# A convolution and MLP kernel: a stream kept less its mean, 320-column banks, more split transforms and a seven-product block

## The chip, the cores and the metric

The kernel runs on one core of a Trainium2 chip. The metric is the device time of one execution in microseconds (us), the median of several runs. The engines are PE (matrix multiply, with PEld for its weight loads), DVE (vector), ACT (scalar), POOL and SP, which issues most DMAs.

## The reference, cut to what matters

```python
x = A_q                                        # 2048 tokens x 640 channels
x = x + A(layernorm(x), k, v, shift_k, ssm_k, ssm_D)
x = x + B(layernorm(x), w1, w2)
x = x + A(layernorm(x), k, v, shift_k, ssm_k, ssm_D)
x = x + B(layernorm(x), w1, w2)

def A(q, ...):
    kv = short_causal_conv(k, shift_k) * v     # 4 taps per channel
    y = causal_conv(kv, ssm_k) + kv * ssm_D    # 2048 taps per channel, over time
    return q * y                               # y does not depend on x
def B(x, w1, w2):                              # 640 -> 1728 -> 640
    return relu(x @ w1) @ w2
```

`y` is the same in both A layers, so it is worked out once.

## The kernel before, in words

**Chunks and blocks.** The 2048 tokens are 8 chunks of 256, each of two halves `s` of 128 tokens (half 1 holds the first 128 tokens in reverse). The MLP runs in blocks `(chunk, layer, halves)`. Chunks 0 and 1 run half by half; chunks 2 to 7 run with both halves in one block, in the order (2,0), (3,0), (2,1), (3,1), (4,0) and so on to (7,1). `main` (L913) emits a block, `prep` (L832) what stands ahead of it: for layer 0 and 1 the A part (statistics, gate with `y`, add) and the layernorm of B, then the split of the normed rows in two fp16 parts and their transposes.

**The MLP.** Each operand is a high and a low fp16 part, and three products (high by high, high by low, low by high) stand for one. `mm1` (L1009) makes `h`, 7 steps `j` of 256 hidden columns; ACT and DVE make relu and its two parts `hh`, `hl` (L1086, L1087); `mm2` (L992) adds into the output: per half one PSUM bank of 512 columns (`o0`, `o1`), and for the last 128 columns of both halves a third (`oc`). DVE adds the bank into the stream `x` (L1177, an instruction of 512 and one of 128 columns for each half). Blocks in `WINO`, which are (7,0), (6,1) and (7,1), use seven products of 320 columns in place of eight for the steps `j` that are not in `plain` (L941; `wprod` L970, `wplain` L959). For layer 0 of a chunk below 7 the first three `j` and the last tail step would be plain. The seven products need sums of quarters of w2 (`wcombine`, L750) and of `h` (L1073 to L1084), both made by ACT and DVE.

**The stream and layernorm.** `stats` (L782) makes the mean and the inverse deviation; ACT writes the normed rows `xn` (L810). For the A part DVE multiplies `xn` by `y` (L851) and adds that to `x` with a running sum (L855). Chunk 0 has a path of its own ("direct", L651 to L667), since its `y` stands at the head of everything.

**The convolution.** It is done chunk by chunk with transforms of length 128 on PE and complex products of chunk pairs on DVE. The work is cut into units of one or two (chunk, channel group) pairs; `SPLIT` says how many units of chunks 2-3, 4-5 and 6-7 take two channel groups of one chunk, the others take one channel group of two chunks ("chunk pairs"), which share the loaded partners. `transform` (L361) makes taps, product, and the transforms `pg` (of the filter) and `pr`; `products` (L550) the sums of products, the back transform `pq` and the store of `y`. A matmul of a transform is either fp32 (L471, L619) or "split": three products of a rounded high part and a rest (`mm3`, L326 to L330), for which ACT and DVE make both parts (L456, L457, L625, L626). `FG` and `FU` are the ranks in the list of units from which `pg` and `pq` are split; before, both are 11, which is the first unit of chunks 4-5.

**The order of the work.** `Plan.order` (L134) is a list scheduler. Each operation has an engine, a cost written by hand, and a class: `CRIT` (head of the kernel), `URGENT` (releases a block), `SOON`, `CONV`, `SPILL`, `LATER`, `FILL` (the MLP's matmuls). Each engine takes the lowest class that is ready and has room in its buffers, and the result is fixed as the engine's order of instructions. Any change of a cost or a buffer thus reorders much of the program. `T` makes a tile in a ring of buffers; the rings of PSUM are `h` (2 banks), `tr` (2, for the transforms), `o0`, `o1`, `oc` and `x` (1 each).

**The head.** While w1 and w2 stream in (28 tiles, L692), PE sums their squares (`pw`, L699) to find a scale for each (`norms`, L682: a diagonal `dg` L704, a small matmul `pn` L706, then `wn`, `wnr`, `wpw`, `wsc`). `wsplit` (L723) then makes the two fp16 parts of each of the 28 tiles, the high part on ACT (L731) and the low part on DVE (L732). "spin" matmuls (L716, L1194) fill PE where nothing else is planned.

Of the kernel before, what the change touches and what calls it, by code (L numbers as in the profile page):

```python
# [21 lines left out]
P = 128  # L22
# [37 lines left out]
FU = 11  # L60
FG = 11
SPLIT = (2, 0, 1)
HALVES = 2
AADD, RADD = (), ()
GADD, SADD = 4, 4
PAIRED = 1
WINO = ((7, 0), (6, 1), (7, 1))
# [8 lines left out]
class Tile:  # L76
    def __init__(self, ring, shape, dtype, name, stream=0):
        self.ring, self.shape, self.dtype, self.name, self.stream = ring, list(shape), dtype, name, stream
        self.t, self.left, self.writer, self.readers = None, 0, None, []
        if ring is not None:  # L80
            ring.lines.setdefault(stream, []).append(self)
# [4 lines left out]
    def r(self, pat, **kw):  # L86
        return self.t.rearrange(pat, **kw)

# [10 lines left out]
class Plan:  # L99
# [5 lines left out]
    def op(self, eng, cost, fn, reads=(), writes=(), prio=0, nbytes=0, late=0.0):  # L105
# [9 lines left out]
        for t in writes:  # L115
            if t.writer is not None:
                deps.add(t.writer)
            elif t.ring is not None and not t.left:
                o.new.append(t)
            deps.update(t.readers)  # L120
# [4 lines left out]
        o.tiles = list({id(t): t for t in (*reads, *writes)}.values())  # L125
# [8 lines left out]
    def order(self):  # L134
# [9 lines left out]
        def fits(o):  # L144
            at = {}
            for t in o.new:
                k = at.setdefault(t.ring, {})
# [14 lines left out]
        while n < len(self.ops):  # L162
# [27 lines left out]
            for e in engs:  # L190
# [17 lines left out]
                for t in best.new:  # L208
                    t.ring.free -= 1
# [23 lines left out]
    def issue(self):  # L233
        out, end = self.order()
        for o in out:
            for t in o.new:
                t.t = t.ring.pool.tile(t.shape, t.dtype, tag=t.ring.tag, name=t.name, bufs=t.ring.bufs)
# [5 lines left out]
def tile_h3_mlp(ctx: ExitStack, tc: tile.TileContext, q, kT, vT, shk, hF, hR, dD, w1, w2, cM, cG, out):  # L243
# [65 lines left out]
    POOL.memset(c15.t, 1.5)  # L309
    shs = keep(const, [P, NDT, 4], "shs")  # L310
# [22 lines left out]
    def pieces(u, ap):  # L333
# [23 lines left out]
        "p0": (ps, "o0", 1, 1),  # L357
        "p1": (ps, "o1", 1, 1),
    }

    def transform(u):  # L361
        ring = ALT if u == [(0, 2), (0, 3)] else MAIN

        def R(k, shape, name):
            pl, tag, bufs, stream = ring[k]
# [184 lines left out]
    def products(u, at, gt, after):  # L550
# [98 lines left out]
        act(h, lambda: ACT.activation(qs.t, pq[:, 256 : 256 + h].rearrange("p (a b) -> p a b", a=n), AF.Copy), [pq], [qs], pr_)  # L649
        pp = lambda: pq[:, 0:h].rearrange("p (a b) -> p a b", a=n)  # L650
        dve(h, lambda: DVE.tensor_sub(yo(0), pp(), qs.t), [pq, qs], [dst[0]], pr_)  # L651
# [11 lines left out]
        if direct:  # L663
            xs, xns, sp0 = first[c]
            for s in range(2):
                dve(h, lambda s=s: DVE.tensor_mul(xns[s][:, cs], xns[s][:, cs], dst[s][:, cs]), [xns[s], dst[s]], [xns[s]], (CRIT, BACK)[s])
                dve(h, lambda s=s: DVE.scalar_tensor_tensor(xs[s][:, cs], xns[s][:, cs], 1.0, xs[s][:, cs], op0=ALU.mult, op1=ALU.add, accum_out=sp0[s][:, 0, t0 // 2 : t0 // 2 + 1]), [xns[s], xs[s]], [xs[s], sp0[s]], (CRIT, BACK)[s], 0.2)  # L667
# [14 lines left out]
    def norms():  # L682
        ones = T(cv, "u", 2, [P, P], "ones", stream=1)
        plan.op("POOL", 0.5, lambda: POOL.memset(ones.t, 1.0), [], [ones], SOON)
        out_ = []
        for k, e in ((0, 9), (1, 13)):
            pw2 = T(ps, *(("h", 2), ("oc", 1))[k], [P, 2, P], f"pw{k}", stream=1)
            for j in JS:
                for i in range(2):
# [5 lines left out]
                    def f(m=2 * j + i, t=t, pw2=pw2):  # L695
                        top = t.t.bitcast(BF16).rearrange("p (n two) -> p n two", two=2)[:, :, 1]
                        for d in range(NDT):
                            x = top[:, d * P : d * P + P]
                            PE.matmul(pw2[:, 0], x, x, start=(m == 0 and d == 0), stop=(m == 2 * JS[-1] + 1 and d == NDT - 1))  # L699
# [4 lines left out]
            dve(P, lambda jk=jk, pw2=pw2, s2=s2: DVE.scalar_tensor_tensor(jk.t, pw2[:, 0], 1.0, ident.t, op0=ALU.mult, op1=ALU.mult, accum_out=s2.t), [pw2, ident], [jk, s2], URGENT, 0.2)  # L704
            pn = T(ps, "x", 1, [P, 512], f"pn{k}", stream=1)
# [73 lines left out]
    def small(tag, name):  # L779
        return T(mlp, tag, 2, [P, 2], name)  # L780

    def stats(xs, sums, name, S, pr=0, fine=False):  # L782
        q_ = slice(S[0], S[-1] + 1)
        negm, ssq, sd, r, v, nmr = (small(k, k + name) for k in ("negm", "ssq", "std", "rstd", "var", "nmr"))
        dve(2, lambda: DVE.tensor_scalar(negm[:, q_], sums[:, q_], -1.0 / D, None, op0=ALU.mult), [sums], [negm], pr)
        for s in S:
# [13 lines left out]
            (0.19 * len(S), [r, negm], [nmr], lambda: [A(nmr[:, c], r[:, c], ident_, scale=negm[:, c]) for c in cols]),  # L800
        ]
        if fine:
            for cost, rd, wr, f in steps:
                act(0, f, rd, wr, pr, cost - 0.1)
        else:
            act(0, lambda: [f() for *_, f in steps], [ssq, sd, negm, heps, c15], [v, r, nmr], pr, sum(x[0] for x in steps))
# [20 lines left out]
    def add_sum(x, t, sums, s):  # L827
        plan.op("POOL", 1.1, lambda: POOL.dma_start(out=x.t, in_=t.t, accum_op=ALU.add), [x, t], [x], URGENT, 8 * D * P)
        if sums is not None:
            act(D, lambda: ACT.activation(t.t, x.t, AF.Copy, accum_out=sums[:, s : s + 1]), [x], [t, sums], URGENT, 0.1)  # L830

    def prep(a, layer, S, pr=0):  # L832
# [4 lines left out]
        if head:  # L837
            xs, _, sp0 = first[a]
# [3 lines left out]
        else:  # L842
# [6 lines left out]
            xns = stats(xs, sums, "A" + nm, S)  # L849
            for s in S:  # L850
                ew("ay", D, lambda e, s=s, xn=xns[s]: e.tensor_mul(xn.t, ys[s].t, xn.t), [ys[s], xns[s]], [xns[s]], URGENT)  # L851
                if (a, layer) in AADD:
                    add_sum(xs[s], xns[s], sums2, s)
                    continue
                dve(D, lambda s=s, xn=xns[s]: DVE.scalar_tensor_tensor(xs[s].t, xn.t, 1.0, xs[s].t, op0=ALU.mult, op1=ALU.add, accum_out=sums2[:, s : s + 1]), [xns[s], xs[s]], [xs[s], sums2], URGENT, 0.2)  # L855
# [24 lines left out]
        else:  # L880
            xns = stats(xs, sums2, "B" + nm, S, pr)
        for s in S if not head else ():
# [16 lines left out]
        for x in range(2):  # L899
            pt = T(ps, f"o{x}", 1, [P, NDT, P], f"xt{nm}{x}", F16, stream=1)  # L900

            def f(x=x, pt=pt):
                for t in range(NDT):
                    PE.transpose(pt[:, t, :], hl[0][x][:, t * P : t * P + P], ident16.t)

            pe(0.29, f, [hl[0][x], ident16], [pt], pr)
            if x:
                dve(D, lambda pt=pt: DVE.tensor_copy(xt[1].t, pt.t), [pt], [xt[1]], pr)
            else:
                act(D, lambda pt=pt: ACT.activation(xt[0].t, pt.t, AF.Copy), [pt], [xt[0]], pr)  # L910
        return xT, S

    def main(n, a, layer, S, xTS):  # L913
# [7 lines left out]
        wino = (a, layer) in WINO  # L921
        if wino:
            bank = [T(ps, tag, bufs, [P, 512], f"o{n}{m}", stream=st) for m, (tag, bufs, st) in enumerate((("o0", 1, 0), ("o1", 1, 0), ("oc", 1, 0), ("x", 1, 3), ("tr", 2, 7), ("tr", 2, 7)))]
        else:
            ob = {s: T(ps, f"o{s}", 1, [P, 512], f"o{n}{s}") for s in S}
            oc = T(ps, *(("x", 1) if n == 1 else ("oc", 1)), [P, 2, P], f"oc{n}", stream=sm)
        o = lambda s, h: oc[:, s] if h else ob[s].t
        ds = (slice(0, H), slice(H, D)) if wino else (slice(0, 512), slice(512, D))
# [63 lines left out]
        def mm2(j, i, hh, hl, SS=S):  # L992
            tail = j == NFP - 1 and i == 1

            def f():
                wh, wl = (WT[j, 1, i][:, k, :] for k in range(2))
                for s in SS:
                    c = slice(i * R + (s - S[0]) * P, i * R + (s - S[0]) * P + P)
                    for h in range(2):
                        d, z = ds[h], o(s, h)  # L1000
                        end = j == JS[-1] and i == 1 and (h == 0 or s == S[-1])
                        PE.matmul(z, hh[:, c], wh[:, d], start=(j == JS[0] and i == 0 and (h == 0 or s == S[0])), stop=False)  # L1002
# [4 lines left out]
            pe(0.136 * (4 if tail else 6) * len(SS), f, [hh, hl, WT[j, 1, i]], [*(ob[s] for s in SS), oc], FILL)  # L1007
# [329 lines left out]
```

## Time and profile before

| | |
|---|---|
| median of 3 runs | 859.96 us (858.65 to 864.69) |
| span of the profiled execution | 858.4 us |
| busy: PE, DVE, ACT | 843.4, 743.1, 482.2 us |
| DMA, mean over the span | 207 GB/s, 178.05 MB |

The profiled execution's own time is its span and what little lies around it: the span is 0.3 us under the lowest of the three runs and 1.6 us under their median. Matmuls are pipelined: the page's duration of one is longer than the distance between the starts of two that follow each other, so what a matmul costs is read from the starts in the order of time.

### The profile page before, as it was taken

The numbers are of one execution on the slowest core, as the hardware profiler recorded it, in microseconds if no ns is written. First come the engines' busy times: TensorE is split into PE (matmuls) and PEld (weight loads), VectorE is DVE, ScalarE is ACT, GpSimd is POOL, SyncE is SP. The second block draws the span as 40 slices with busy tenths as digits, with TensorE's granted clock in tenths as the row PEclk, the third lists the DMA queues.
The fourth block names the chain that finished last, engine by engine and source line by source line (L and its number), as shares of the span: only waits on it lengthen the run. The fifth ranks groups of instructions, "written<-read, shape, count | busy, mean of one in ns | idle before, by whom it ended". The sixth has DMA issues, their size and how long they took to land.

```text
span 858.4 us, 19690 instructions
## 1 busy us (share of the span) xinstructions
PE 843.4 (98%) x7808; PEld 663.1 (77%) x7808; DVE 743.1 (87%) x1367; ACT 482.2 (56%) x1121; POOL 46.5 (5%) x57
## 2 busy tenths in 40 slices
PE   8989999999999999999999999999999999999997
PEld 7867877777878777777777777878777777888886
DVE  7999999999889999999999999999897575645543
ACT  6597586455686375728448383835416275727331
POOL 2000000000011001101010000001000000000000
PEclk9999999999999999999999999999999999999999
DMA  9994968798999979889788988687985562110100
GB/s 325 391 296 150 270 192 287 213 340 281 310 260 284 325 192 270 201 255 252 197 245 243 223 236 168 184 189 241 266 272 200 135 216 31 44 20 2 43 20 32
DMA packets 133838, 178.05 MB, mean 207 GB/s; under 512 B 50545, under 2 KB 87153, under 8 KB 133746
## 3 DMA queue, kind: packets, MB, share of 16 engines
q1 hardware_dynamic: 125426, 166.31, 62.5%
q0 software_dynamic: 8320, 10.49, 8.1%
q8 instruction: 61, 1.00, 0.5%
q14 instruction: 31, 0.25, 0.1%
HBM read 122.03 MB, written 34.08 MB: 182 GB/s over the span
## 4 chain that ended last, share of the span: by engine, by line
PE 81%; DVE 10%; DMA 4%; ACT 3%; issue 2%; SPq 1%; DVEq 0%; ACTq 0%
PE h L1030 12%; PE h L1033 12%; PE h L1031 12%; PE o L1003 8%; PE o L1002 8%; PE o L1005 7%; PE o L957 7%; PE oc L1003 2%; PE oc L1002 2%; PE oc L1005 2%; DMA A<-at 1%; PE pq L619 1%; DVE pd L596 1%; PE hb L1030 1%; PE hb L1031 1%
## 5 line engine op out<-in xcount | busy, mean ns | idle before, releaser
L1030 PE MATMUL h<-xT,w 128*128 128x256 f16 (+1 forms) x1290 | 301.5, 252 | 0.7 <-DVE hh L1087 0.6
L1033 PE MATMUL h<-xT,w 128*128 128x256 f16 (+1 forms) x1290 | 301.3, 251 | 0.4 <-DVE w L732 0.4
L1031 PE MATMUL h<-xT,w 128*128 128x256 f16 (+1 forms) x1290 | 301.3, 251 | 0.0
L1031 PEld LDWEIGHTS <-w 128*128 128x128 f16 x1390 | 136.0, 98 | 11.2 <-issue 1.0
L1030 PEld LDWEIGHTS <-w 128*128 128x128 f16 x1390 | 135.9, 98 | 10.4 <-ACT w L737 0.2
L1003 PE MATMUL o<-w,hh 128*128 128x512 f16 x364 | 137.9, 379 | 0.4 <-DVE w L732 0.4
L1002 PE MATMUL o<-w,hh 128*128 128x512 f16 x364 | 138.1, 379 | 0.0
L1033 PEld LDWEIGHTS <-w 128*128 128x128 f16 x1290 | 126.2, 98 | 9.8 <-DVE w L732 0.6
L597 DVE TENSOR_TENSOR pacc<-pacc,pd 128x768 f32<-128x768 f32 x140 | 133.0, 950 | 0.5
L1003 PEld LDWEIGHTS <-hh 128*128 128x128 f16 x728 | 71.2, 98 | 45.8
L1002 PEld LDWEIGHTS <-hh 128*128 128x128 f16 x728 | 71.2, 98 | 44.6 <-issue 0.2
L1086 ACT ACTIVATE hh<-h 128x512 f16<-128x512 f32 (+1 forms) x103 | 50.4, 489 | 97.7 <-PE h L1033 94.4
L1005 PE MATMUL o<-w,hl 128*128 128x512 f16 x234 | 88.7, 379 | 0.0
L1003 PE MATMUL oc<-w,hh 128*128 128x128 f16 x364 | 79.7, 219 | 0.0
L1002 PE MATMUL oc<-w,hh 128*128 128x128 f16 x364 | 79.7, 219 | 0.0
L596 DVE TENSOR_TENSOR pd<-Ax,Gx 128x768 f32<-128x768 f32 x83 | 77.8, 951 | 0.9 <-DMA Gx<-G 0.8
L1005 PEld LDWEIGHTS <-hl 128*128 128x128 f16 x468 | 45.8, 98 | 27.6
L1005 PE MATMUL oc<-w,hl 128*128 128x128 f16 x234 | 51.2, 219 | 0.0
L394 ACT ACTIVATE tp<-kt,shs 128x256 f32<-128x256 f32 (+1 forms) x78 | 42.7, 574 | 13.0 <-DVE acc L431 10.8
L1087 DVE SCALAR_TENSOR_TENSOR hl<-h,hh 128x512 f16<-128x512 f32 x55 | 37.6, 685 | 11.0 <-ACT hh L1086 11.0
L596 DVE TENSOR_TENSOR pd<-at,Gx 128x768 f32<-128x768 f32 x46 | 43.2, 951 | 0.6 <-DMA Gx<-G 0.5
L412 POOL DMA_DIRECT2D gs<-hr x20 | 19.6, 980 | 387.5 <-DVE pacc L593 189.1
(232 smaller groups left out, 1666.6 us busy)
## 6 DMA issues: line engine op xcount, KB each, us to landing
Ax<-A SPq DMA_DIRECT2D x89, 384.0 KB, 4.5
Gx<-G SPq DMA_DIRECT2D x89, 384.0 KB, 4.1
G<-gt SPq DMA_DIRECT2D x30, 384.0 KB, 5.2
A<-at SPq DMA_DIRECT2D x30, 384.0 KB, 4.6
y<-Y SPq DMA_DIRECT2D x30, 320.0 KB, 4.7
ws<-in_w SPq DMA_DIRECT2D x28, 320.0 KB, 6.6
x<-in_q SPq DMA_DIRECT2D x16, 320.0 KB, 5.5
out_dram<-x SPq DMA_DIRECT2D x16, 320.0 KB, 4.0
```

The costliest lines, as they stand in the source:

```text
L394: ACT.activation(o[:, i : i + m], kview(i, m, j), AF.Copy, scale=shs[:, t, j : j + 1])
L596: ew(f"mac{j % POOLMOD}", 768, lambda e, pd=pd, av=av, gv=gv: e.tensor_mul(pd.t, av(), gv()), [ax, gx], [pd], pr_)
L597: dve(768, lambda i=i, pd=pd: DVE.tensor_add(acc[:, i], acc[:, i], pd.t), [acc, pd], [acc], pr_)
L957: PE.matmul(b[:, c : c + w], x, y[:, z : z + w], start=done[i] == 1, stop=done[i] == total[i])
L1002: PE.matmul(z, hh[:, c], wh[:, d], start=(j == JS[0] and i == 0 and (h == 0 or s == S[0])), stop=False)
L1003: PE.matmul(z, hh[:, c], wl[:, d], start=False, stop=end and tail)
L1005: PE.matmul(z, hl[:, c], wh[:, d], start=False, stop=end)
L1030: PE.matmul(p[:, z], wh, xv(t, 0), start=b, stop=False)
L1031: PE.matmul(p[:, z], wh, xv(t, 1), start=False, stop=tail and e)
L1033: PE.matmul(p[:, z], wl, xv(t, 0), start=False, stop=e)
L1086: act(2 * R, lambda p=p, hh=hh: ACT.activation(hh.t, p.t, AF.Relu), [p], [hh], URGENT)
L1087: dve(2 * R, lambda p=p, hh=hh, hl=hl: DVE.scalar_tensor_tensor(hl.t, p.t, 0.0, hh.t, op0=ALU.max, op1=ALU.subtract), [p, hh], [hl], URGENT)
```

## The change

1. **Stream less its mean.** `x + xn * y`, with `xn = (x + negm) * r` (`negm` is minus the mean, `r` the inverse deviation), becomes `(x + negm) * (1 + r * y)`: ACT writes `1 + r * y`, one DVE instruction does the rest. The stream then lacks its mean, which is kept in small tiles (`MEAN`) and added back by ACT in layer 1 after the layernorm. The direct path of chunk 0 is changed in the same way, and `negm` moves from DVE to ACT.
2. **320-column banks.** `o0`, `o1`, `oc` and `x` become two rings `oA` and `oB` of one tile with two banks each; `mm2` writes 320 columns into either bank, and one DVE instruction of 640 columns adds both to the stream.
3. **`FU`, `FG` 11 to 8:** the last three units of chunks 2-3 use split transforms.
4. **`SPLIT` (2, 0, 1) to (2, 0, 0):** chunks 6 and 7 are all in chunk pairs.
5. **`WINO` gains (6, 0):** a fourth block with seven products, in the steps 3, 4 and 5 only (the rest is plain there). The units of chunk 7 and `wcombine` are now called for ahead of (6,0), no longer ahead of (7,0).
6. Options that were off (`AADD`, `RADD`, `add_sum`) are removed; the small rings get 4 buffers in place of 2.

```diff
-FU = 11
-FG = 11
-SPLIT = (2, 0, 1)
+FU = 8
+FG = 8
+SPLIT = (2, 0, 0)
...
-WINO = ((7, 0), (6, 1), (7, 1))
+WINO = ((6, 0), (7, 0), (6, 1), (7, 1))
...
+    def banks(tag, name, stream=0, shape=(512,), dtype=F32):
+        x = T(ps, tag, 1, [P, 2, *shape], name, dtype, stream)
+        return [Bank(x, k) for k in range(2)]
...
-        act(h, lambda: ACT.activation(qs.t, pq[...], AF.Copy), [pq], [qs], pr_)
-        dve(h, lambda: DVE.tensor_sub(yo(0), pp(), qs.t), [pq, qs], [dst[0]], pr_)
+        if direct:
+            xs, (negm, rs, nrs), qx, sp0 = first[c]
+            for s in range(2):
+                f = (nrs, rs)[s]
+                act(h, ... ACT.activation(qv(s), pm(), AF.Identity, scale=f[:, s : s + 1], bias=one.t), ..., (CRIT, BACK)[s], 0.09)
+                dve(h, ... DVE.scalar_tensor_tensor(qv(s), pp(), rs[:, s : s + 1], qv(s), op0=ALU.mult, op1=ALU.add), ..., (CRIT, BACK)[s], 0.13)
+                dve(h, ... DVE.scalar_tensor_tensor(xs[s][:, cs], xs[s][:, cs], negm[:, s : s + 1], qx[s][:, cs], op0=ALU.add, op1=ALU.mult, accum_out=...), ..., (CRIT, BACK)[s], 0.2)
+        act(h, lambda: ACT.activation(qs.t, pm(), AF.Copy), [pq], [qs], BACK if direct else pr_)
...
-        if direct:
-            xs, xns, sp0 = first[c]
-            for s in range(2):
-                dve(h, ... DVE.tensor_mul(xns[s][:, cs], xns[s][:, cs], dst[s][:, cs]), ..., (CRIT, BACK)[s])
-                dve(h, ... DVE.scalar_tensor_tensor(xs[s][:, cs], xns[s][:, cs], 1.0, xs[s][:, cs], ...), ..., (CRIT, BACK)[s], 0.2)
...
+        pw1, pn = banks("oB", "pw1", 2)
         for k, e in ((0, 9), (1, 13)):
-            pw2 = T(ps, *(("h", 2), ("oc", 1))[k], [P, 2, P], f"pw{k}", stream=1)
+            pw2 = pw1 if k else T(ps, "h", 2, [P, P], "pw0", stream=1)
...
-            pn = T(ps, "x", 1, [P, 512], f"pn{k}", stream=1)
...
-        dve(2, lambda: DVE.tensor_scalar(negm[:, q_], sums[:, q_], -1.0 / D, None, op0=ALU.mult), [sums], [negm], pr)
+        act(2, lambda: ACT.activation(negm[:, q_], sums[:, q_], AF.Copy, scale=-1.0 / D), [sums], [negm], pr, 0.1)
...
-                ew("ay", D, lambda e, s=s, xn=xns[s]: e.tensor_mul(xn.t, ys[s].t, xn.t), ..., URGENT)
-                dve(D, ... DVE.scalar_tensor_tensor(xs[s].t, xn.t, 1.0, xs[s].t, op0=ALU.mult, op1=ALU.add, accum_out=...), ..., URGENT, 0.2)
+                act(D, ... ACT.activation(qx.t, ys[s].t, AF.Identity, scale=r[:, s : s + 1], bias=one.t), ..., URGENT, 0.09)
+                dve(D, ... DVE.scalar_tensor_tensor(xs[s].t, xs[s].t, negm[:, s : s + 1], qx.t, op0=ALU.add, op1=ALU.mult, accum_out=...), ..., URGENT, 0.2)
+            keepm(a, negm, S)
...
+            if layer:
+                for s in S:
+                    act(D, lambda s=s: ACT.activation(xs[s].t, xs[s].t, AF.Identity, bias=MEAN[a][:, s : s + 1]), ..., URGENT, 0.1)
...
-            ob = {s: T(ps, f"o{s}", 1, [P, 512], f"o{n}{s}") for s in S}
-            oc = T(ps, *(("x", 1) if n == 1 else ("oc", 1)), [P, 2, P], f"oc{n}", stream=sm)
-        ds = (slice(0, H), slice(H, D)) if wino else (slice(0, 512), slice(512, D))
+        ob = {s: banks(("oA", "oB")[s], f"o{n}{s}") for s in S}
+        ds = (slice(0, H), slice(H, D))
...
-            for h in range(2):
-                    DVE.scalar_tensor_tensor(xs[s][:, d], o(s, h), fac[s].t, xs[s][:, d], op0=ALU.mult, op1=ALU.add, **acc)
+                DVE.scalar_tensor_tensor(xv_, ob[s][0].whole[:, :, 0:H], fac[s].t, xv_, op0=ALU.mult, op1=ALU.add, **acc)
```

More of the change, by code (lines that the diff above doesn't have):

```diff
@@ L805, in stats @@
         else:
[L806 removed]
+            act(0, lambda: [f() for *_, f in steps], [ssq, sd, negm, heps, c15], [v, r] + [nmr] * (nmr is not None), pr, sum(x[0] for x in steps))
+        if gate_:
+            return negm, r, nmr
         xns = {}
```

139 lines of the change are left out of this document (79 added, 60 removed).

## The prediction

> **What bounds the kernel now.** First the page: the span, the busy shares and the slices.
>
> ```profile
> span 858.4 us, 19690 instructions
> PE 843.4 (98%) x7808; PEld 663.1 (77%) x7808; DVE 743.1 (87%) x1367; ACT 482.2 (56%) x1121; POOL 46.5 (5%) x57
> DVE  7999999999889999999999999999897575645543
> ```
>
> PE is busy for 843.4 of 858.4 us, so 14.9 us are left in which it has nothing to do. The view by stretches tells where they lie (columns: stretch, its length, then PE, PEld, DVE, ACT, POOL busy, the granted clock, the DMA share, GB/s).
>
> ```profile
> 0.00:20.00 20.00, 16.66 (x112) 15.09 (x113) 13.87 (x29) 12.44 (x27) 4.37 (x17) 1.00 0.92 320
> 20.00:40.00 20.00, 19.35 (x243) 18.17 (x242) 18.15 (x58) 10.06 (x26) 0.00 (x0) 1.00 1.04 389
> 40.00:60.00 20.00, 17.77 (x237) 14.69 (x237) 19.35 (x38) 19.61 (x39) 0.00 (x0) 1.00 1.03 345
> 60.00:80.00 20.00, 19.19 (x209) 13.99 (x207) 19.86 (x43) 15.21 (x30) 0.00 (x0) 1.00 0.38 125
> 140.00:160.00 20.00, 19.57 (x226) 16.03 (x224) 18.92 (x36) 13.97 (x37) 0.00 (x0) 1.00 0.73 234
> 160.00:180.00 20.00, 17.92 (x196) 14.13 (x195) 18.92 (x32) 7.01 (x17) 0.00 (x0) 1.00 0.97 308
> 220.00:840.00 620.00, 619.94 (x5405) 480.31 (x5403) 527.76 (x927) 335.96 (x780) 40.24 (x38) 1.00 0.68 189
> 840.00:858.40 18.40, 13.09 (x129) 10.88 (x126) 8.48 (x20) 2.67 (x5) 0.00 (x0) 0.94 0.10 37
> ```
>
> PE idles 3.34 + 0.65 + 2.23 + 0.81 = 7.0 us before 80, 0.43 + 2.08 = 2.5 us between 140 and 180, 0.06 us in the 620 us from 220 to 840, and 5.3 us at the end, where the last block is added and stored. So three limits follow each other: the head, where DVE is at 18 to 19.9 of 20 us; the long middle, where only matmul work counts; and an end that the change leaves alone (the instruction order of both programs ends with the same operations). In the middle a microsecond taken from DVE or ACT is worth nothing by itself. What is worth something is a matmul less.
>
> **The change part by part: matmul work.** The price of a matmul is the distance between starts. In order of time (start, length, instruction):
>
> ```profile
> 205.98 1.08 PE L619 MATMUL pq<-u,cM 128*128 128x256 f32 x4
> 206.90 0.38 PE L1002 MATMUL o<-w,hh 128*128 128x512 f16 x1
> ...
> 313.24 0.28 PE L329 MATMUL pq<-ul,cMh 128*128 128x256 f32 x1
> 314.41 0.27 PE L330 MATMUL pq<-uh,cMl 128*128 128x256 f32 x1
> ...
> 654.63 0.38 PE L1002 MATMUL o<-w,hh 128*128 128x512 f16 x1
> 655.44 0.38 PE L1002 MATMUL o<-w,hh 128*128 128x512 f16 x1
> ...
> 732.70 0.43 PE L957 MATMUL o<-wt,hh 128*128 128x320 f16 x2
> 732.97 0.30 PE L957 MATMUL o<-wt,hl 128*128 128x320 f16 x1
> ```
>
> *Split transforms.* An fp32 matmul leaves two records; four of them, two matmuls, take 0.92 us up to the next start, 0.46 a matmul, in which the change from one kind to another is counted; I take 0.43, the lower end. The split form takes three: from 313.24 to 314.41 lie ten steps, 0.117 each, so 0.35. Three units, two transforms each (`pg` and `pq`), four matmuls each: 24 x (0.43 - 0.35) = **-1.9 us** (-2.6 by 0.46). DVE pays for it with 12 more differences of 512 (0.684 each, below: +8.2 us), ACT with 12 more casts; they fall between 150 and 240 us, where PE's only idle of the middle lies, and are weighed there.
>
> *320-column banks.* A pair of 512 and 128 columns three times over takes 655.44 - 654.63 = 0.81, so 0.27 for a pair; 320 columns take 0.27 / 2 = 0.135, so two of them 0.27. **0 us** on PE; the number of matmuls is the same.
>
> *Seven products in (6,0).* In the steps 3, 4 and 5, 24 matmuls of 320 columns become 21: 3 x 3 x 0.136 = 1.2 us less; 38 more of the matmuls that are cut in 192 + 128 columns cost some 3 ns each: **-1.1 us**. The work that it adds on DVE (per step four sums of 128, two differences; then some 12 instructions in place of two to empty the banks) comes to about 12 us and lies in the stretch where the page's slices show DVE at half load (the last ten slices).
>
> *Chunk pairs for 6 and 7.* Same five units, same matmuls; 24 loads of 384 KB fewer. DMA is no limit in that stretch: **0 us**.
>
> **DVE and ACT work.** Rows of the groups by shape (busy us, mean ns behind the bar):
>
> ```profile
> L851 DVE TENSOR_TENSOR xnA<-y,xnA 128x640 f32<-128x640 f32 x30 | 24.0, 820 | 3.4 <-ACT xnA L810 2.4 <-DMA y<-Y 0.9
> L626 DVE TENSOR_TENSOR ul<-u,uh 128x512 fp32r<-128x512 f32 x20 | 13.7, 684 | 0.7 <-ACT uh L625 0.6
> L1177 DVE SCALAR_TENSOR_TENSOR x<-o,winv,x 128x512 f32<-128x512 f32 x24 | 17.9, 745 | 2.4 <-PE o L1005 2.4
> L1177 DVE SCALAR_TENSOR_TENSOR x<-oc,winv,x 128x128 f32<-128x128 f32 x24 | 8.3, 345 | 2.3 <-PE oc L1005 2.3
> L773 DVE SCALAR_TENSOR_TENSOR wt<-wc,wsc,wt 128x1280 f16<-128x1280 f32 x4 | 6.2, 1552 | 4.4 <-ACT wt L772 4.4
> ```
>
> 30 products of 0.82 go (-24.6). 745 and 345 ns lie 384 columns apart, 1.04 ns a column, so one of 640 takes 0.88 in place of 1.09: with two halves fewer, -7. `negm` moves to ACT (-5). Against it +8.2 (split) and +12 (seven products): DVE loses about 17 us of 743. ACT gains 16 adds of a mean (about 0.9 each by L810's kind of instruction) and the casts, and stays under two thirds. By the bound above none of it counts from 220 on. From 80 to 220 DVE has some 10 halves of A parts at -0.8 and the narrower emptying at -0.2, against +8.2 for the splits, so a little is won, and I take **-0.8 us** of the 2.5 us idle there. Ends: +2 (the splits push `hl` back and PE waits as at 160 to 180 once more) and -2.5 (all idle goes).
>
> **The head.** What starts block (0,0) are the transposed rows and the first split tiles of w1:
>
> ```profile
> 35.82 0.15 DVE L710 TENSOR_SCALAR wsc<-wpw 128x1 int32<-128x1 int32 x1
> 36.75 0.55 DVE L865 TENSOR_SCALAR xc<-x,negmB 128x640 f32<-128x640 f32 x1
> 38.94 0.29 DVE L704 SCALAR_TENSOR_TENSOR dg<-pw,ident 128x128 f32<-128x128 f32 x1 [1.64 <-PE pw L699]
> 41.07 0.88 DVE L869 SCALAR_TENSOR_TENSOR xl<-xc,rstdB,xh 128x640 f16<-128x640 f32 x1
> ...
> L732 DVE SCALAR_TENSOR_TENSOR w<-ws,wsc,w x28: 867/878/885, 39.2 to 71.3; 128x640 f16<-128x640 f32 x28
> ...
> 42.29 0.22 PE L1018 MATMUL h<-xT,w 128*128 128x128 f16 x1
> ```
>
> The direct path needs two DVE instructions after ACT for half 0 in place of three, and the work for `y` itself is put behind; `cMl`, the first `dg` and one sum no longer stand in DVE's way. By the order, `xc` comes about 2 us earlier, at 34.6. But the order also puts the `pn` matmul of w1 behind the last `pw` of w2, which waits for the last weight tile (38.9 here), and DVE takes `wn`, then the second `dg`, before `xl` and before w1's scale. So the scale, at 35.82 before, comes at about 40.5; then ACT makes the first high part (0.8), the copy of the transposes, the second high part, DVE the low parts: the first `mm1` starts near 43.8 in place of 42.3, **+1.5**. Then DVE has 28 splits of 0.80 (22.4) and 12.6 us of other work in its order up to the last split, 35.0 us from 38.9: last split out at about 74, before 72.1. That it does not cost 2 us more is due to the order on PE: the transforms of chunk 1 (`pg`, 1.7 us) and two steps of `mm1` for half 1 (3.4 us), whose rows are ready earlier, now stand between the first `mm1` and the `mm2` that wait for w2's splits. Going down PE's order with these times, it has done the same amount of matmul work at 79.7 as before at 80.9: **-1.2 us** for the whole head. Ends: +4 (the first matmul late and nothing won back) and -4 (also the idle between 40 and 80 shrinks by most of its 3.0).
>
> **Sum.** -1.9 - 1.1 - 0.8 - 1.2 = -5.0: the profiled execution's 858.4 becomes 853.4. It lies 1.6 us under the median of 859.96, so I forecast **855.0** (-0.6%). A measurement of this kernel can tell about 1% from no change.
>
> One rule speaks against the split. Loading a matrix of 128 columns for it has this row:
>
> ```profile
> L330 PEld LDWEIGHTS pq<-uh,cMl x40: 187/188/189, 313.2 to 676.9; 128*128 128x128 f32 x40
> ```
>
> [...] By weight loads the split costs: 12 loads of 0.188 per transform against 8 of 0.190, +0.74 us x 6 = +4.4 us. The trace does not agree that loads set the pace here: split matmuls start 0.117 apart, less than one load lasts, and LDWEIGHTS is busy for 77% while PE's starts leave no gap.
>
> **The rivals.**
> 1. *Weight loads bound PE* (the rule just weighed): the split then gives +4.4 in place of -1.9. 855.0 + 6.3 = 861.3. Against it stand the starts 0.117 apart in 313 to 314. Chance 0.03.
> 2. *The head gets slower* (the other side). DVE's order puts `wn`, which waits for the last weight tile, ahead of all it needs for block (0,0). If PE cannot use the other work in between, because `h` has only two banks and its reader `hl` stands behind the splits on DVE, then the end of the splits sets the head: +1.9 there and another +1.5 to 3 of PE's wait for the first `mm1`, about +4.5. 855.0 + 5.7 = 860.7. It decides from a head 3.8 us longer than before. For it: DVE at 19.35 of 20 from 40 to 60. Chance 0.12.
> 3. *The matmuls saved come back as waits*: 8 us more DVE work between 150 and 240, where DVE has 18.9 of 20, makes `pg` and `hl` late. +3 in place of -0.8: 858.8. Chance 0.17.
> 4. *DVE's relief clears the idle time*: all of the 2.5 us, and 3 more of the head. 855.0 - 1.7 - 3 = 850.3. For it: both stretches wait on DVE. Against it: the first wait of the head is one for DMA. Chance 0.14.
> 5. *(6,0) waits for its sums*: `wcombine` (six times four sums of 0.49 and one row L773, 21 us of DVE) must be done by step 3 of (6,0). By the order, PE has 71 us of work between the last `pq` and that step, so it should fit; if not, some 10 us: 865 to 870. Chance 0.04.
>
> **How the numbers follow.** The forecast has 0.50. Its own range is 852 to 857.5. The range from 850 to 861 takes in rivals 2, 3 and most of 4, with the bounds of the head (+4, -4) and of the middle. Faster by over 1% means under 851.4: most of rival 4 and a little of the forecast, 0.16. Slower by over 1%, over 868.6: part of rival 5 and what I do not see, 0.05. Within 1%: 0.79.
>
> **What would show it.** Right: 12 split matmuls at 0.117 apart for units of chunks 2 and 3; PE idle of 0.1 us or less per 100 us after 240; the first `mm1` of block (0,0) near 43.8 and PE idle before 80 at 6 to 8 us; PE's busy time near 840. Wrong: a first `mm1` after 46, PE waits on `hl` or `pg` between 150 and 240 of over 4 us, or gaps in block (6,0).

## The result, and the profile after

The changed kernel takes 857.84 us in the median of 20 runs (856.51 to 861.41), the kernel before, run beside it, 860.85 (858.65 to 864.69): ratio 0.9965, 95% interval 0.9956 to 0.9974, or 3.0 us less. 855.0 had been forecast (-0.6%), with 850 to 861 as range.

The page of the changed kernel begins so:

```profile
span 856.9 us, 19812 instructions
PE 842.0 (98%) x7878; PEld 710.7 (83%) x7878; DVE 731.4 (85%) x1295; ACT 505.3 (59%) x1188; POOL 47.0 (5%) x58
```

This execution took 859.45 us, 1.6 more than the median; why is seen in the head below. DVE lost 11.7 us (17 forecast). PEld, the weight loads, is busy for 48 us more while the time fell, and split matmuls still start 0.12 us apart (below): rival 1 is out. The stretches that answer to those shown of before:

```profile
0.00:20.00 20.00, 17.13 (x111) 15.16 (x112) 13.72 (x28) 12.53 (x29) 4.74 (x18) 1.00 0.91 316
20.00:40.00 20.00, 18.51 (x202) 16.60 (x201) 18.64 (x56) 10.10 (x30) 0.00 (x0) 0.96 1.04 391
40.00:60.00 20.00, 19.11 (x271) 17.41 (x270) 17.70 (x37) 17.95 (x36) 0.00 (x0) 0.95 0.91 297
60.00:80.00 20.00, 20.00 (x207) 16.29 (x205) 19.73 (x37) 16.93 (x31) 0.00 (x0) 1.00 0.46 173
140.00:160.00 20.00, 19.22 (x217) 16.23 (x216) 19.94 (x36) 15.16 (x38) 0.00 (x0) 1.00 0.86 284
160.00:180.00 20.00, 19.69 (x225) 17.13 (x223) 20.00 (x33) 8.63 (x19) 0.00 (x0) 1.00 0.95 311
220.00:840.00 620.00, 617.81 (x5444) 516.40 (x5443) 517.10 (x873) 353.38 (x827) 42.26 (x40) 1.00 0.65 175
840.00:856.90 16.90, 11.63 (x113) 9.52 (x110) 8.54 (x20) 2.29 (x5) 0.00 (x0) 0.92 0.10 39
```

PE's idle time went from 7.0 to 5.25 us before 80, from 2.5 to 1.1 between 140 and 180, stayed at 5.3 in the end, rose from 0 to 1.1 between 80 and 140, and rose from 0.06 to 2.2 us in the long middle from 220 on, which was forecast to stay as it was. Two columns are new there: the granted clock (the third last) is 0.96 and 0.95 in the head, and DVE is at 19.94 and 20.00 of 20 us from 140 to 180.

To compare the work itself I value every matmul by its distance to the next start where nothing waits (0.056 us for 128 columns, 0.136 for 320, 0.118 for a split one of 256, two records of 0.216 for one in fp32) and add up all of them: 833.4 us before, 830.4 after, **2.9 us less** before rounding, against 3.0 forecast. The split matmuls come as forecast, here in a `pg` at 162 us:

```profile
162.90 0.28 PE L355 MATMUL pg<-gh,cGl 128*128 128x256 f32 x1
163.02 0.28 PE L353 MATMUL pg<-gh,cGh 128*128 128x256 f32 x1
163.14 0.28 PE L354 MATMUL pg<-gl,cGh 128*128 128x256 f32 x1
163.26 0.28 PE L355 MATMUL pg<-gh,cGl 128*128 128x256 f32 x1
```

So the time fell by 3.0 us and the matmul work by 2.9, which looks like an answer: only matmul work counts. The experiments show that it is a coincidence of larger terms.

**The wait in the middle.** PE's longest wait after 80 us, with ACT's and POOL's instructions around it (the brackets hold the idle time ahead of an instruction and what ended it):

```profile
269.16 0.75 ACT L421 ACTIVATE tp<-kt,shs 128x512 f32<-128x512 f32 x1
272.66 0.63 ACT L438 ACTIVATE hr<-hr 128x512 f32<-128x512 f32 x1 [2.76 <-DMA gs<-hr]
273.20 0.37 ACT L1132 ACTIVATE hh<-h 128x256 f16<-128x256 f32 x1
```

```profile
264.65 0.91 POOL L439 DMA_DIRECT2D gs<-hr  x1 [1.56 <-issue]
```

```profile
273.62 0.31 PE L1048 MATMUL o<-w,hh 128*128 128x320 f16 x1 [1.55 <-ACT hh L1132]
```

L438 changes the sign of `hr` in place and has to wait for the accumulating transfer that reads `hr`; issued at 264.65, it lets L438 start at 272.66, 8 us later, where the planner's model has 1.1 us after its bytes. The `hh` that PE needs wants nothing from that transfer; it only stands behind L438 in ACT's queue. PE idles 1.55 us for it, 1.7 counted between undisturbed starts.

### The profile page after: what moved, and what is told of

Read it like the earlier page. It is cut to its first block, busy times and chain, and to the rows that moved or that the text cites. A ratio compares the mean times of both kernels' runs of the same rounds, so it can differ in the third digit from the quotient of the medians.

```text
span 856.9 us, 19812 instructions
## 1 busy us (share of the span) xinstructions
PE 842.0 (98%) x7878; PEld 710.7 (83%) x7878; DVE 731.4 (85%) x1295; ACT 505.3 (59%) x1188; POOL 47.0 (5%) x58
## 4 chain that ended last, share of the span: by engine, by line
PE 74%; DMA 8%; DVE 8%; ACT 6%; issue 2%; SPq 1%; DVEq 0%; POOLq 0%; ACTq 0%
PE h L1076 11%; PE h L1077 11%; PE h L1079 11%; PE o L1003 9%; PE o L1048 8%; PE o L1049 8%; PE o L1051 7%; DMA ws<-in_w 2%; DMA gs<-hr 2%; DMA gs<-in_hF 1%; DMA hf<-in_hF 1%; PE hb L1077 1%; PE hb L1076 1%; DVE pd L623 1%; DVE w L763 1%
## 5 line engine op out<-in xcount | busy, mean ns | idle before, releaser
L1048 PE MATMUL o<-w,hh 128*128 128x320 f16 x672 | 200.3, 299 | 1.6 <-ACT hh L1132 1.6
L1049 PE MATMUL o<-w,hh 128*128 128x320 f16 x672 | 200.0, 299 | 0.4 <-DVE w L763 0.4
L1077 PEld LDWEIGHTS <-w 128*128 128x128 f16 x1390 | 136.0, 98 | 15.1 <-issue 1.2
L1051 PE MATMUL o<-w,hl 128*128 128x320 f16 x416 | 124.4, 299 | 0.0
L1132 ACT ACTIVATE hh<-h 128x512 f16<-128x512 f32 (+1 forms) x100 | 48.4, 484 | 66.7 <-PE h L1079 57.1
L1048 PEld LDWEIGHTS <-hh 128*128 128x128 f16 x672 | 65.7, 98 | 24.2 <-ACT hh L1132 1.9
L1049 PEld LDWEIGHTS <-hh 128*128 128x128 f16 x672 | 65.8, 98 | 21.8
L1051 PE MATMUL o<-w,hh 128*128 128x320 f16 x208 | 62.2, 299 | 1.0 <-DVE hh L1133 0.9
L1051 PEld LDWEIGHTS <-hl 128*128 128x128 f16 x416 | 40.7, 98 | 15.8
L1003 PE MATMUL o<-w,hh 128*128 128x192 f16 (+2 forms) x312 | 42.2, 255 | 0.0
L1133 DVE SCALAR_TENSOR_TENSOR hl<-h,hh 128x512 f16<-128x512 f32 x52 | 35.6, 685 | 5.7 <-ACT hh L1132 5.4
L1119 ACT ACTIVATE ha<-h 128x512 f32<-128x512 f32 x20 | 11.8, 589 | 48.0 <-PE h L1079 48.0
L1123 DVE TENSOR_TENSOR hs<-ha 128x128 f32<-128x128 f32 x20 | 5.8, 290 | 38.5 <-ACT ha L1119 38.5
```

Of the source, the lines that this page charges most:

```text
L1003: PE.matmul(b[:, c : c + w], x, y[:, z : z + w], start=done[i] == 1, stop=done[i] == total[i])
L1049: PE.matmul(z, hh[:, c], wl[:, d], start=False, stop=end and tail)
L1051: PE.matmul(z, hl[:, c], wh[:, d], start=False, stop=end)
L1077: PE.matmul(p[:, z], wh, xv(t, 1), start=False, stop=tail and e)
L1132: act(2 * R, lambda p=p, hh=hh: ACT.activation(hh.t, p.t, AF.Relu), [p], [hh], URGENT)
L1133: dve(2 * R, lambda p=p, hh=hh, hl=hl: DVE.scalar_tensor_tensor(hl.t, p.t, 0.0, hh.t, op0=ALU.max, op1=ALU.subtract), [p, hh], [hl], URGENT)
```

## The experiments

Theory A, which takes from the prediction the terms that add up to the measured 3.0: only matmul work counts; the gain is the split's 1.9 and block (6,0)'s 1.1. Rival B: the gain is DVE's relief between 80 and 220 us. All ratios are to the kernel before on the same chip.

**1 to 3: the parts one by one.** Edits of the changed kernel:

```
e1  FU, FG = 11, 11                            (no more split units)
e2  WINO = ((7, 0), (6, 1), (7, 1))            (block (6,0) by eight products)
e3  both of these, and SPLIT = (2, 0, 1)       (stream and banks alone)
```

> The changed kernel with the three more units back in fp32 (FU and FG 11); the other parts stay. Theory A (only matmul work counts: the gain of 3.0 us, from 860.85 to 857.84, is the split's 1.9 and block (6,0)'s 1.1): the sum of matmul work rises by 1.9 us and the time goes to 859.8, a ratio to the kernel before of 0.9987. Theory B (the gain comes from DVE's relief in 80 to 220 us, and the split uses part of it up as waits): without the split's 12 differences there is less waiting, and the time stays at 857.8 or falls, ratio 0.9965 or less.

> The changed kernel with block (6,0) by eight products again; the other parts stay. Theory A: matmul work rises by 1.1 us and the time goes to 858.9, ratio 0.9978; the wait of 0.62 us at 687 us goes, so 858.3 if that wait was due to the sums. Theory B: the seven products in (6,0) gave nothing, since DVE's sums before them cost what they save: 857.8, ratio 0.9965.

> The stream less its mean and the 320-column banks alone: no further split, old units for chunks 6 and 7, block (6,0) by eight products. Theory A: matmul work is that of the kernel before; DVE's 25 us less count for nothing in the middle, and the head is as long as before: ratio 1.000 (0.999 to 1.001), 860.8. Theory B: DVE's relief is worth 1.5 us or more in 80 to 220 us: ratio 0.998 or less.

Measured: e1 858.22 us, 0.9954 (0.9941 to 0.9967); e2 858.12, 0.9965 (0.9952 to 0.9979); e3 858.59, 0.9963 (0.9950 to 0.9976). The stream and the banks alone give the whole gain, though their matmul work, 833.4 us, is that of the kernel before. Theory A falls. e1 comes out as its theory B has it (0.9965 or less), and e2 at the number of its own: the 1.1 us of block (6,0) do not show in the time, within an interval of about 1.1 us to either side. The stream and the banks are not told apart by any run. Yet the 2.9 us less are there in the changed kernel: so something in it takes them back. e1 and e3 have the instruction order of the changed kernel up to about 150 us and a new one from there on, e2 up to block (6,0). Of e2, which has the split, the waits of PE and of ACT between 262 and 280 us (total, times, longest):

```profile
PE o L1048 <- ACT hh L1132: 1.6, 1, 1.6
```

```profile
ACT hr L438 <- DMA gs<-hr: 2.8, 1, 2.8
```

In e1 and e3, without the split, that view lists no wait of PE and none of L438. So the split's 1.9 us seem to come back as the wait at 273 us; e6 and e10 test that.

**4: w1's scale early.** `pn` of w1 ahead of the last eight weight tiles' `pw`, by one dependency more:

```
-                    pe(5 * 0.057, f, [t], [pw2], SOON)
+                    pe(5 * 0.057, f, [t] + [pn] * (k == 1 and j in JS[-2:]), [pw2], SOON)
```

> The changed kernel with one dependency more, which puts the pn matmul of w1 ahead of the last eight weight tiles' pw matmuls, so that w1's scale no longer waits for w2's last tile. Theory C (the late scale makes the head 2.5 us longer than it need be): scale near 38.5 in place of 41.3, first mm1 near 42.5 in place of 44.9, and the time falls by 2 us, to 855.8, ratio 0.9942. Theory D (other work on PE and DVE's chain of splits cover it, the head is bound by DVE until 74 us): first mm1 earlier, PE work done at 80 us the same within 0.5, time 857.8, ratio 0.9965.

Measured: 859.51, 0.9977 (0.9968 to 0.9985), slower than the changed kernel. Its profile can't be set beside the others, so where the time lies isn't shown; e11 tries the same again.

**5: the product back.** One instruction more in each A part:

```
+ dve(D, lambda qx=qx: DVE.tensor_tensor(qx.t, qx.t, qx.t, op=ALU.max), [qx], [qx], URGENT)
```

> The stream and the banks alone (as in e3, ratio 0.9963), with one DVE instruction of 640 columns more in each half of every A part outside the head: a maximum of q with itself, which changes no value and stands in place of the product that the stream took away (30 times 0.82 us, 24.6 us of DVE). Theory B (the gain of 3.0 us is DVE's relief outside the head, in 80 to 220 us): DVE is back at about 742 us and the time at 860.5, ratio 0.999. Theory E (the gain is in the head, where this instruction does not stand, or in the banks): time as in e3, 858.6, ratio 0.9963; lost time of PE before 80 us about 10 us, after it as in e3.

Measured: 865.99, 1.0045 (1.0026 to 1.0064): 7.4 us over e3, where B had 860.5, 1.9 over it. The direction is that of B, the size is almost four times its own. The planner gives every engine a new order for it, and the longest wait is one that e3 does not have:

```profile
PE h L1077 <- DMA xT<-xh: 2.3, 1, 2.3
```

**6 to 8: three edits by way of the planner.** e6 tells the planner that an accumulating transfer takes 7 us; e7 and e8 put six spins behind the last `pw` steps, e8 with e4's dependency.

```
e6  -  end = dma + 1.1
    +  end = dma + (1.1 if e == "SP" else 7.0)
e7  +  for _ in range(6 * (k == 1 and j in JS[3:])):
    +      PE.matmul(spin2[:, 0:P], ident16.t, ident16.t, start=True, stop=True)
    ...    (the step's price in the plan rises to match)
```

> The changed kernel, with the order's model of an accumulating transfer on POOL's queue set from 1.1 to 7 us after its bytes, so that ACT's L438, which waits for the first one, is put behind more of the hh that PE needs. In the changed kernel and in e2 (both with the split) PE waits 1.7 us at 273 us for an hh that stands behind L438; in e1 and e3 (both without) it does not. Theory F (the split's 1.9 us are real, and come back as this wait): the wait goes, and the time falls by 1.7 us against the changed kernel, to 856.1, ratio 0.9946. Theory G (the lost time only moves elsewhere): ratio 0.9965.

> The changed kernel with six matmuls on the identity behind each of the last eight weight tiles' pw matmuls, which fill PE where it waits for the weight tiles. In the changed kernel the granted clock is at half for 3.4 us from 38.4 us. Theory H (that costs PE 1 to 1.7 us of work, and more in the runs with a lower mean clock): mean clock 0.999 or more, and the time falls by 1 us, to 856.8, ratio 0.9953. Theory I (in that time PE waits for ACT and DVE anyway): clock up, time the same, ratio 0.9965.

> As the run before, and also w1's pn matmul ahead of the last eight weight tiles' pw matmuls, as in e4 (0.9977 alone, which is slower than the changed kernel). Theory C (the early scale helps once the clock is not at half): first mm1 before 43 us, time 855.5, ratio 0.9938. Theory D (the head hangs on DVE's chain; an early scale puts the splits ahead of other work that is needed sooner): 857.8 or slower, ratio 0.9965 to 0.998.

Measured: 872.43, 870.14 and 871.25 us; 1.0118 (1.0087 to 1.0149), 1.0093 (1.0064 to 1.0121), 1.0109 (1.0078 to 1.0140). All expectations missed by over 10 us, and for a reason that none named: each edit changes the planner's times, and with them the order of the whole program. In e6 the wait at 273 is gone, and 12 us are lost elsewhere, in one wait for transposed rows, with the clock at half for 13.65 us during and behind it:

```profile
PE h L1076 <- DMA xT<-xh: 12.1, 1, 12.1
```

In e7 the planner put `pn` of w1 so early that PE's queue stood for 3.44 us, and from 35.7 us on the clock was at half for 6.8 us (stretches of e7):

```profile
37.51 0.58 PE L739 MATMUL pw<-ws,ones 128*128 128x1 f32 x2 [3.44 <-DVE dg L738]
```

```profile
34.00:36.00 2.00, 0.07 (x1) 0.00 (x0) 1.86 (x8) 0.97 (x3) 0.00 (x0) 0.93 1.04 390
36.00:38.00 2.00, 0.49 (x3) 0.49 (x4) 1.55 (x11) 1.22 (x3) 0.00 (x0) 0.50 1.05 386
38.00:40.00 2.00, 2.00 (x21) 2.00 (x22) 1.84 (x8) 0.92 (x2) 0.00 (x0) 0.50 1.09 355
40.00:42.00 2.00, 2.00 (x22) 2.00 (x20) 1.50 (x5) 1.62 (x3) 0.00 (x0) 0.50 1.06 403
```

So a cost of a few us can't be told in this kernel by an edit that the planner sees. From here on the planned order is kept, and single operations are moved in it by hand.

**9: the product back, order kept.** The extra instruction stands in the closure of the one behind it, so that the planner does not see its price; the order on PE, ACT, POOL and SP is that of e3 instruction by instruction.

```
- dve(D, lambda ...: DVE.scalar_tensor_tensor(xs[s].t, ...), ...)
+ dve(D, lambda ...: (DVE.tensor_tensor(qx.t, qx.t, qx.t, op=ALU.max), DVE.scalar_tensor_tensor(xs[s].t, ...)), ...)
```

> As e5 (the stream and the banks alone, with the product's 24.6 us of DVE put back outside the head), but the extra instruction stands in the same step of the plan and the planner does not see its price, so that the order on every engine is that of e3. It tells what DVE's relief is worth by itself, apart from the order, which changed in e5 on every engine. Theory B (the relief in 80 to 220 us is the gain): ratio 0.999, 860.5. Theory J (e5's 865.99 came from its other order; DVE's time outside the head is worth nothing): ratio 0.9963 as e3, 858.6.

Measured: 873.36, 1.0147 (1.0129 to 1.0165), 14.8 us over e3 for 24.8 us of DVE. The two middle stretches of e3, then of e9:

```profile
80.00:220.00 140.00, 138.19 (x1521) 119.14 (x1520) 136.03 (x249) 90.21 (x232) 1.88 (x2) 1.00 0.85 267
220.00:840.00 620.00, 618.85 (x5383) 514.32 (x5381) 501.65 (x829) 346.73 (x818) 40.23 (x38) 1.00 0.69 187
```

```profile
80.00:220.00 140.00, 133.62 (x1439) 114.69 (x1437) 134.08 (x241) 87.90 (x227) 1.88 (x2) 0.99 0.82 254
220.00:840.00 620.00, 612.02 (x5328) 506.49 (x5326) 524.64 (x857) 344.77 (x816) 40.24 (x38) 1.00 0.70 190
```

PE's idle time grows by 4.6 us between 80 and 220, as B has it, and by 6.8 us after 220, where DVE is busy for 85% and PE had been idle for 1.15 of 620 us. Counted against undisturbed starts it is 6.4 and 8.9 us, together near the 15.1 us by which the span grew (856.9 to 872.0); 1.6 us of the 6.4 are a stretch of 3.4 us at half clock from 153 us on. So DVE time that is put into a given order counts in the whole middle, also where PE had hardly been idle, and theory J is refuted. Two things stay open. The extra instruction stands in the chain from `y` to the next block as well as in DVE's queue, and the run doesn't tell which of the two costs. And e9 puts time in: that time taken *out* after 220 would gain something isn't shown, since the kernel before, with the product in its plan, has 0.06 us of idle time there to win. The prediction's sentence that a microsecond taken from DVE in the middle is worth nothing by itself is thus not refuted for 220 to 840; what fails is its use for work that is added or moved.

**10: one pair on ACT changes places**, in the changed kernel's own order:

```
+    def move(self, out):
+        neg = [o for o in out if o.name == "neg"][1]
+        hh = next(o for o in out[out.index(neg) + 1 :] if o.eng == "ACT")
+        out.remove(neg)
+        out.insert(out.index(hh) + 1, neg)
...
```

> The changed kernel in its own order, but for one pair on ACT: the second L438 and the hh behind it change places, so that this hh no longer waits behind L438 for an accumulating transfer. All else stands as it was (e6 tried it by the planner's price, and the order changed everywhere). Theory F (the split's 1.9 us are real, and 1.7 of them come back as this wait): the wait at 273 us goes, ratio 0.9945, 856.1. Theory G (what follows waits in its place, as PE's next operands hang on the same transfer): ratio 0.9965, 857.8.

Measured: 854.02, 0.9926 (0.9913 to 0.9939). ACT in e10, and its stretch from 220 to 300 us:

```profile
268.80 0.38 ACT L1142 ACTIVATE hh<-h 128x256 f16<-128x256 f32 x1 [0.57 <-PE h L1089]
271.49 0.64 ACT L447 ACTIVATE hr<-hr 128x512 f32<-128x512 f32 x1 [2.30 <-DMA gs<-hr]
```

```profile
220.00:300.00 80.00, 80.00 (x868) 69.32 (x867) 76.53 (x128) 58.84 (x154) 9.40 (x9) 1.00 0.98 285
```

L438 (L447 here) still waits 2.3 us, but nothing that PE needs stands behind it, and PE is busy for 80.00 of 80 us (78.26 in the changed kernel). Theory F holds: 0.9926 to 0.9965 is 3.4 us, by the ends of the two intervals 1.5 to 5.2, where 1.7 had been forecast. Between the two profiles the span falls by 4.1 us: about 1.3 of it are the head, where the changed kernel's profile was at half clock and e10's was not (below), 1.7 are this wait, and 0.4 a wait at 687 us, which is gone as well. And this wait is not the same in each execution: in e11, with the same ACT order there, it is 3.8 us, and the clock is at half for 6.8 us behind it. Against e1, which has fp32 in place of the split and an order of its own, e10 is 0.0028 or 2.4 us faster, near the split's 1.9.

**11: the head by hand.** Some 40 operations between the last weight tile and the first `mm1` (w1's scale first, transposes ahead of the spins, five spins in each of the `pw` steps before):

```
+        put("DVE", ["rec0", "wn0", "wpw0", "wsc0", "dg1", "sums1", "negm1", "wn1", "xl0", "wl0_00", "xTl", "wl0_01", ...], "dg0")
+        put("ACT", ["wnr0", "xh0", "wh0_00", "xTh", "wh0_01", "wnr1", "sq1"], "std0")
...
```

> The changed kernel in its own order, but for the 40 or so operations between the last weight tile and the first mm1: pn of w1 ahead of the last weight tile's pw, the scale of w1 and its first split ahead of what half 1 and w2 need, the transposes no longer behind 31 spins, and five spins in each of four pw steps ahead. Expected: scale at 38.6 (41.3 in the changed kernel), first mm1 at 41.5 (44.9), granted clock 1.0 there. Theory C (the late first mm1 costs): PE's work done at 80 us rises by 2 us or more, time 855.4, ratio 0.9937. Theory D (DVE's chain of splits decides, and it starts as late as before): first mm1 earlier, the work done at 80 us the same within 0.5, ratio 0.9965.

Measured: 859.15, 0.9984 (0.9973 to 0.9996), slower than the changed kernel. PE's work done by 80 us, counted as above, fell to 65.2 us (66.8 in the changed kernel, 68.1 in e10); 0.3 of it are six spins fewer. The scale came at 40.5, not 38.6, as `wn` waits for the last `pw` of w2 too, which shares its tile; and what the scale was moved ahead of was late in turn: PE stood 1.06 us for `gs` at 47.85. (`xc`, ahead of all that was moved, came 1.2 us later in this execution, at 38.08, and the execution took 862.73 us, 3.6 over the median, so its numbers are not those of the ordinary one.) In this execution the wait at 273 was there at its longest, and ACT's wait ahead of it too:

```profile
PE o L1123 <- ACT hh L1207: 3.8, 1, 3.8
```

```profile
ACT hr L487 <- DMA gs<-hr: 5.1, 1, 5.1
```

Theory C is not borne out, but not tested in full either, as the scale came 0.8 us earlier and not 2.7. The clock was at 1.00 from 36 to 44, so it was not the clock of the head.

**12: four operations on DVE.** As e10, with what stands ahead of them on DVE put behind them:

```
+ AHEAD = (("hl2_5", 2), ("hl3_3", 1), ("hl3_6", 1), ("ys2_0", 1))
...
```

> As e10 (ratio 0.9926), and on DVE four operations that PE waits for in 130 to 162 us change places with what stands ahead of them: the low half of an activation tile ahead of an A sum and a product (PE waits 0.95 us at 130.7 in e10), another ahead of a filter sum (0.64 at 150.2), a third ahead of a row split (0.45 at 153.9), and the sum that frees a PSUM bank ahead of a product (0.54 at 161.2). Everything else stands in its order. Theory K (waits that remain in the middle are places in an in-order queue, as at 273 us): most of the 2.6 us go, ratio 0.9903, 852.0. Theory L (DVE is short of time there, at 136.0 of 140 us busy, so what is put back is waited for next): the waits move, ratio 0.992 to 0.994.

Measured: 854.99, 0.9928 (0.9907 to 0.9949), as e10. The waits move: PE's idle time between 80 and 220 is 1.9 us in place of 2.1, and the longest wait that is left, at 132 us, is one that e10 does not have, for an operation close behind the first exchange:

```profile
PE pr L372 <- DVE ys L708: 0.6, 1, 0.6
```

with DVE at 19.83 and 19.97 of 20 us in 140 to 180. The number is that of theory L: DVE has no time left there, and these four exchanges do not help. The fastest version is e10: by the ratios 6.4 us less than the kernel before and 3.4 less than the changed one, whose ratio was measured in other runs.

## Why the prediction was right, and where it was wrong

The time lay in its range, 2.8 us above the value: 0.9 because the kernel before measured 860.85 and not 859.96, the rest because the change is worth 3.0 and not 5.0. The range from 850 to 861 also holds the time of the kernel before, so that to lie in it says little; the steps say more: one failed, and two came out with a wrong size or by a wrong path.

- *Matmul work, -3.0.* Right: -2.9. e10, in which the wait that came with the split is gone, shows that the split is worth its time; for block (6,0)'s 1.1 no run shows it (e2).
- *320-column banks 0, chunk pairs 0.* As matmul work the banks are 0 (e3 has the 833.4 us of before); in the time neither was tested alone, so that is open.
- *DVE loses 17.* It lost 11.7. The products (-24.0 for 30), the emptying (17.9 + 8.3 before, 19.3 after) and the splits (+7.8) came as priced; the instruction that adds and multiplies in the A parts takes 881 ns where the one before took 818, and the rest is spread over small ones.
- *80 to 220, -0.8.* PE's idle there went from 2.56 to 2.15 us, the time lost against undisturbed starts from 4.9 to 4.0: -0.9. Right.
- *The head, -1.2.* The work of the matmuls that ended by 80 us is 66.8 before and 66.8 after, so 0 in the profiled execution. But e2, e3, e5, e6, e9, e10 and e12, with the same order up to there, have done 68.0 to 68.3: -1.2 to -1.5. (e1, with that order too, has done 67.2; its clock was at half for 3.4 us from 8.7 us on.) What differs is the clock, first in the changed kernel, then in e10:

```profile
38.00:40.00 2.00, 1.86 (x19) 1.87 (x20) 1.81 (x7) 1.03 (x3) 0.00 (x0) 0.60 1.09 359
40.00:42.00 2.00, 2.00 (x22) 2.00 (x21) 1.07 (x8) 0.64 (x2) 0.00 (x0) 0.54 1.06 394
```

```profile
38.00:40.00 2.00, 1.64 (x22) 1.47 (x23) 1.53 (x9) 1.42 (x5) 0.00 (x0) 1.00 1.09 359
40.00:42.00 2.00, 2.00 (x38) 2.00 (x39) 1.67 (x8) 1.28 (x3) 0.00 (x0) 1.00 1.06 402
```

  At half clock the 31 spins ahead of the transposes start 0.107 us apart in place of 0.056, and the first `mm1` starts at 44.89; in e10 it starts at 43.47, where 43.8 was forecast:

```profile
44.89 0.22 PE L1064 MATMUL h<-xT,w 128*128 128x128 f16 x1
```

```profile
43.47 0.22 PE L1074 MATMUL h<-xT,w 128*128 128x128 f16 x1
```

  So the step was right for an execution whose clock stays full, in part by luck: `xc` came at 36.83 (37.36 in e10), not 34.6. Eight instructions of the direct path with a scalar per row start 0.40 us apart (0.33 for a plain sum of 256 columns), which by an estimate from these two makes 0.6 us; the rest of that error I can't place. It did not carry over, since w1's scale, on which the first `mm1` hangs as well, came at 40.66 in e10, near the 40.5 forecast (41.30 at half clock).
- *From 220 on, 0.* Wrong. This is the step that failed: "By the bound above none of it counts from 220 on". PE's idle there rose from 0.06 to 2.2 us, 1.7 of it at 273. A stretch without idle time had been read as one in which the other engines have time to spare. It was without idle time in the order that the planner had laid out for just that work. With the split the order changed, and L438 came to stand ahead of an `hh` (in e1 and e3, without the split, it does not). Rival 3, "the matmuls saved come back as waits", priced this (+3 on the way to 858.8), but looked for it on DVE between 150 and 240. The other 0.45 us are at 687, where an `hl` stands behind 1.55 us of `wcombine` on DVE, a trace of rival 5; e10, with the same order on PE and DVE, does not have this wait, so it hangs on the times as well.

```profile
687.01 0.31 PE L1003 MATMUL o<-w,hl 128*128 128x192 f16 x2 [0.45 <-DVE hl L1133]
```

- *The other rivals.* Rival 2, a slower head: PE's idle time before 80 fell from 7.0 to 5.25 us, and the first `mm1` came before the 46 named as its sign. Rival 4, all idle time gone: 2.15 us are left between 80 and 220, and 857.84 is far from its 850.3.

The sum between the two profiled executions is -2.9 (work) + 0 (head) - 0.9 + 2.1 = -1.7, and their spans differ by 1.5 (858.4 and 856.9). With the head at full clock it is -2.9, against -3.0 in the medians. That these agree to 0.1 is in part luck: before's span of 858.4 lies under the median spans of that kernel in the later runs (858.8 to 859.8), and the changed kernel's 856.9 is 1.0 over the median of its own (855.9). (The 1.6 us by which the time of before lies over its span are no sign of a short execution: in the later runs of both kernels the time is 1.8 us over the span in the median.) For e3 the same sum gives 0 - 1.2 - 1.7 + 1.2 = -1.7, and its profiled span is 1.5 under that of before; the -3.2 measured (-4.3 to -2.1) are against runs of before whose median span is 859.8, 1.4 more. The prediction had -0.8 - 1.2 = -2.0 for these parts. Put together, e3's -3.2 and the work's -2.9 make -6.1; e10, without the waits at 273 and 687, measures -6.4 (-7.5 to -5.2), and the prediction had -5.0.

## What to carry to other kernels

An engine without idle time says that its feeders are in time, not that they have time left: look at how busy they are in that stretch (DVE 85% here) and what stands behind each wait in their queues, and price an edit that adds to them as a risk of waits. Where a planner sets the order, an edit changes every engine's order; keep the order and move single operations to learn what one thing costs, and then look for instructions that wait for a transfer with something urgent behind them.

## What the runs showed of the hardware

- A granted clock of half came in one execution and not in others with the same order up to there: in the changed kernel for 3.41 us from 38.4 us on (0.60 from 38 to 40, 0.54 from 40 to 42), not there in e1, e2, e3, e5, e6, e9, e10 and e12. Other stretches at half clock lasted 3.4 us (e1 from 8.7 us, e9 from 153), 6.8 (e7 from 35.7, e8 from 34.5, e11 behind the wait at 273) and 13.65 (e6, during and behind its wait of 12.1).
- Ahead of five of these stretches PE had little work. By the undisturbed distances, the matmul work that starts in the 3.41 us ahead was 1.31 us in the changed kernel (from 35.0), 0.44 in e7 (from 32.3), 1.22 in e1 (from 5.3), 1.11 in e9 (from 150) and 1.09 in e11 (from 271, with the wait at 273). In e10 the two stretches of that length around 36 us held 2.50 and 2.63, and the clock stayed full from 36 to 46. That the lack of work brings the half clock is my reading of these numbers; no run shows it by itself.
- In one execution half clock followed on the wait at 273, so that it cost more than its length: in e11, where it is 3.8 us, 6.8 us at half clock came behind it. In the changed kernel's profile it is 1.55 us, 1.63 us of work start in the 3.41 us around it (from 270.5), and the clock stays at 1.00 behind it; in e2's it is 1.6, with 1.50 us of work. How often half clock follows in the changed kernel's other executions isn't shown.
- L438, which rewrites the source of an accumulating transfer of 256 KB, had waited 2.76 us for it when it started at 272.66 us, 8 us after POOL had issued the transfer (264.65), while the DMA engines were busy for 95% of the time (220 to 300 us). In e11 the same instruction waited 5.1 us.
- ACT started nothing while L438 waited: it stood still for 2.76 us, L438 started at 272.66 and the `hh` behind it at 273.20. In e10, with these two exchanged, the `hh` starts at 268.80 and L438 (L447 there) at 271.49.
